# A written-out order of work: its clock refitted, its pacing table refined, its opening reordered

## The chip, the cores and the metric

The kernel runs on one core of a Trainium2 chip. A core has five engines with instruction queues of their own: TensorE (PE: matmuls, with weight loads shown apart as PEld), VectorE (DVE), ScalarE (ACT), GpSimd (POOL) and SyncE (SP, which here issues nearly all DMAs). Each engine works through its queue strictly in the order in which the program was written and waits, at the head of the queue, for semaphores that others raise. The metric is the device time of one execution in microseconds (us), smaller being better.

## The reference

The input `x` has 8192 rows of 448 numbers. Two branches start from its layernorm, and their product is added to `x`:

```python
def _A_ref(x, w1, b1, w2, b2):          # a spectral layer
    Xf = rfft2(x, axes=(1, 2))           # H = 1, so an FFT along the 8192 rows
    z = Xf.reshape(B, H, Wf, NB, BS)     # 4 blocks of 112 channels
    hr = relu(zr @ w1[0] - zi @ w1[1] + b1[0]);  hi = relu(zi @ w1[0] + zr @ w1[1] + b1[1])
    or_ = hr @ w2[0] - hi @ w2[1] + b2[0];       oi_ = hi @ w2[0] + hr @ w2[1] + b2[1]
    or_, oi_ = softshrink(or_, 0.01), softshrink(oi_, 0.01)
    return irfft2(or_ + 1j * oi_)

def _B_ref(x, w_gate, w_up, w_down):     # a GLU: 448 -> 1792 -> 448
    return (_gelu(x @ w_gate) * (x @ w_up)) @ w_down

xn = _layernorm(x)
return x + _A_ref(xn, ...) * _silu(_B_ref(xn, ...))
```

## The kernel before

All products are made in float16 from operands split into a high and a low half, three matmuls for each product, and the larger products go through a scheme of sums and differences (seven products in place of eight) whose operands DVE, ACT and POOL prepare.

**Stages.** The 8192 rows are worked off in 16 chunks of 512 (`NG`), the 1792 hidden columns in two passes `p` of 8 and 6 tiles of 128 (`PF`). The opening (`begin`, `begin1`, `weights`, `ffn`) takes chunks 0 and 1 with plain products (`plain`): for each hidden tile `f`, 22 matmuls of 512 columns, which need the split of that tile's weights (`gu_split`, event `("w", f)`). Chunks 2 to 15 of pass 0 and all of pass 1 use the seven-product form (`chunk`, `unit`, then `down` or `down2`). Between these products PE gets the matmuls of the spectral layer: the first FFT stage (`stage1`), the block MLP of phase 2 (`group`), the last stage of phase 3 (`tiles3`).

**The opening's weights.** `WS` is a ring of three buffers (tile `wst`) of 17 x 128 floats a partition. `begin` takes one for tile 0, `weights` one for tile 1, `gu_loads` one for each later tile. A first-round load (`in_gu`) fills only 8 x 128 of the 17 x 128, 512 KB in all, and the buffer comes free (`WS.put`) when `gu_split` has read it. Hidden tiles are grouped in blocks `BLK` with one power-of-two scale each: tile 0, tile 1, then pairs. The scale of a block needs the largest weight of both its tiles: DVE reduces each tile (`fm` or `fx`), PE turns the result (`bd<-ident,fx`), DVE reduces it (`mxr`), PE spreads it (`bd<-ident,mxr`), DVE computes the scale (`fx`, `fh`, `fc`, `fe`), and only then can ACT write the high halves (`wt<-wst,fc`). A block begins after the scales of the block before it. The second round (`gu_combs`, loads `in_raw`, 1088 KB each) prepares the seven-product form of the same tiles (`gu_comb`).

**Chunk 1 stage.** `chunk1(c)`, started at `T1 + (c - 2) * DT` of the planner's time, makes layernorm, the split and the sums of chunk c (`factors`), and writes them to the DRAM buffer `xts`; `xt_load` brings them back transposed (`DMA_TRANSPOSE xta<-xts` and `xtb<-xts`, issued by SP), and the seven-product part of chunk c starts on PE when its `xta` has landed.

**What sets the order.** The whole program is written by a planner that runs when the kernel is built. `Pace` keeps a clock: tasks are Python generators in a heap by time; each `V.`, `S.`, `G.`, `T.` or `Q.` call goes through `Pace.issue`, which computes when the operation would start (`start`: the engine is free, `ready`: operands are written, plus 0.12 us) and end (`cost`: a formula by engine, width and source), notes that, and emits the instruction. So the planner's times decide only one thing on the chip: which instruction stands before which in each queue. `Pace.clear` holds optional work back while the engine is late or a due instruction is near. `Either.call` (used as `B`, DVE or POOL) estimates the end on both engines and takes POOL when `ends[1] + self.by < ends[0]`, with `by = 0`. The cost model knows that a DVE operation with two SBUF inputs and a POOL operation collide (`port`): the later one is charged what is left of the earlier one. `STEPS` is a table by planner time: a value for DVE or ACT pacing, one added to the landing of DMAs (second value; third for `clear`), and a factor on the estimated durations of ACT, DVE and POOL. `END2` and `END3` spread phases 2 and 3 over fixed planner times and are not touched.

**The start of the opening.** SP issues x rows 0 and 2, weight tile 0 (512 KB), x rows 1 and 3. PE runs 13 matmuls on ones (`keep(13, 512)`, tile `gl`), whose results are overwritten, then waits. In `begin`, DVE's queue is: statistics of rows 0 and 2 (`moments`), the reduction of both halves of weight tile 0 in one instruction, the statistics of row 3, the `mxr` reduction, `normal(0)` and `normal(2)`, then the scale, the two low halves, and the copy of the first transposed rows; the copy of the second is ACT's.

Of the kernel before, what the change touches and what calls it, by code (L numbers as in the profile page):

```python
# [42 lines left out]
STEPS = ((0, 2.75, 0.05, 1), (100, 2.5, 0.15, 1.05), (175, 3, 0.2, 0.98), (250, 2.75, 0.05, 1), (325, 2.5, 0.05, 1), (400, 3.0, 0.1, 1.04), (475, 2.5, 0.05, 1), (550, 3.5, 0.05, 1), (700, 3.25, 0.3, 1), (775, 3.0, 0.3, 0.995), (850, 2.75, 0.05, 0.96), (925, 2.75, 0.05, 1.06), (1150, 2.5, 0.15, 0.995), (1450, 3, 0.1, 0.99), (1525, 2.75, 0.05, 1.02))  # L43
# [6 lines left out]
class Event:  # L50
    def __init__(self):
        self.done, self.waiting = False, []


class Pace:
# [4 lines left out]
    def __init__(self):  # L60
        self.now, self.last, self.n, self.heap = 0.0, 0.0, 0, []
        self.free, self.seen, self.dma = {"SP": 0.7, "ACT": 0.7, "DVE": 0.7, "POOL": 0.7, "PE": 1.0}, {}, 1.75
        self.port = {"DVE": [], "POOL": []}
        self.due = {"DVE": [], "ACT": []}
        self.late = False

# [72 lines left out]
    def ready(self, ap, write, engine):  # L139
        name, lo, hi = self.region(ap)  # L140
        return max((t + 0.12 for a, b, w, t, e in self.seen.get(name, ())
                    if (write or w) and e != engine and a < hi and lo < b), default=0.0)

    def note(self, ap, write, t, e):
# [4 lines left out]
        was.append((lo, hi, write, t, e))  # L149

    def quiet(self, ap):
        return max((x[3] for x in self.seen.get(ap.tensor.name, ())), default=0.0)

    def start(self, e, out, ins):
        outs = [out] if out.space != bass.MemoryType.DRAM else []
        ins = [i for i in ins if i.space != bass.MemoryType.DRAM]
        return outs, ins, max([self.now, self.free.get(e, 0.0)] + [self.ready(i, False, e) for i in ins]
                              + [self.ready(o, True, e) for o in outs])

    def issue(self, e, op, out, ins, run):  # L160
        outs, ins, start = self.start(e, out, ins)
        if e == "SP" or op == "dma_start":
            size = (outs or ins)[0].nbytes()
            self.dma = max(self.dma, start) + size / (320e3 if start > 10.0 else 400e3)
            if start < 10.0:
                self.free[e] = start + 0.46
                end = self.dma + 0.9
            elif op == "dma_start_transpose":
                self.free[e] = start + 1.15 + size / 380e3
                end = max(self.free[e] + 2.6, self.dma + 1.5)  # L170
            else:
                self.free[e] = start + 0.5
                end = max(start + 2.2 + size / 240e3, self.dma + 1.5) + (self.step(start)[1] if outs and start > 100.0 else 0.0)
        else:
            end = start + self.cost(e, op, start, out, ins) * (1.0 if e == "PE" else self.step(start)[3])
            self.free[e] = end
            if self.shares(e, op, out, ins):
                self.port[e] = self.port[e][-11:] + [(start, end)]
        for i in ins:
            self.note(i, False, end, e)  # L180
        for o in outs:
            self.note(o, True, end, e)
# [15 lines left out]
    def shares(self, e, op, out, ins):  # L198

        n, sb, psum = self.wide(out, ins)  # L200
        return e == "POOL" or e == "DVE" and n >= 32 and not psum and (sb >= 2 or op == "tensor_scalar" and sb > 0)

    def cost(self, e, op, start, out, ins):
# [8 lines left out]
        if e == "POOL":  # L212
            t = 0.7 if n < 8 and op == "tensor_tensor_pow" else 0.2 + 0.0023 * n
        elif n < 32:
            return 0.17
        elif psum or sb < 2 and op != "tensor_scalar":
            half = psum == len(ins) == 1 and op == "tensor_copy" and ins[0].dtype == F16
            return 0.14 + (0.00054 if half else 0.00107) * (n + 60 * (extra > 0))
        else:
            t = (0.12 + 0.00112 * n if sb >= 2 else 0.15 + 0.0008 * n) + 0.06 * (extra > 0)  # L220
        other, ahead = ("POOL", 0.15) if e == "DVE" else ("DVE", 0.0)
        return t + max([b - start - ahead for a, b in self.port[other] if a <= start < b] + [0.0])
# [17 lines left out]
class Either:  # L240
# [5 lines left out]
    def __getattr__(self, op):  # L246
        def call(out, *args):
# [4 lines left out]
            return getattr(self.engines[ends[1] + self.by < ends[0]], op)(out, *args)  # L252
# [249 lines left out]
def afno_geglu_kernel(ctx, tc, x, gu, raw, wd, mlp, b1, b2, c_m, c_mt, c_small, c_rows, out):  # L502
# [126 lines left out]
    WS = ring(wp, [128, SL * 128], F32, "wst", 3)  # L629
# [197 lines left out]
    T1, DT = 85.0, 34.5  # L827


    def gu_loads(fs, again):  # L830
        for f in fs:
            t = yield from WS.get()
            if f < 4 and not again:
                yield 2.5 + 2.5 * f

            n = (SL if again else 8) * 128
            Q.dma_start(t[:, 0:n], (raw if again else gu)[f])
            EV["wst", f, again] = t if again else t[:, 0:n].rearrange("p (s c) -> p s c", s=8)
# [51 lines left out]
    def gu_block(b):  # L890
# [23 lines left out]
        for i in range(n):  # L914
# [5 lines left out]
            WS.put(t)  # L920
# [1522 lines left out]
    def begin():  # L2443

        w = yield from WS.get()
# [12 lines left out]
        Q.dma_start(w[:, 0:8 * 128], gu[0][:, 0:8 * 128])  # L2458
# [14 lines left out]
        keep(13, 512)  # L2473
# [6 lines left out]
        t = EV["wst", 0, 0] = w[:, 0:8 * 128].rearrange("p (s c) -> p s c", s=8)  # L2480
# [48 lines left out]
        def leave1(a, b):  # L2529
# [4 lines left out]
            def rest():  # L2534
# [3 lines left out]

        moments(0)
# [4 lines left out]
        V.tensor_reduce(mx, t[:, 0:8].rearrange("p (i k) f -> p i (k f)", i=2), axis=AXIS.X, op=ALU.max,  # L2544
                        apply_absolute_value=True)
# [10 lines left out]
        normal(0)  # L2556
        cast(0, 0, xss[0])
        normal(2)
        cast(0, 2, xss[1])
        variance(1)  # L2560
        variance(3)
        root(2, 2)
        turn(banks[0], 0, xss[0], 0)
# [3 lines left out]
        turn(banks[1], 2, xss[1], 0)  # L2567
# [192 lines left out]
```

## Time and profile before

| | us |
|---|---|
| median of 3 runs (lowest, highest) | 1761.59 (1759.45, 1762.22) |
| profiled execution, device time | 1758.21 |
| its span, first to last instruction | 1756.4 |
| PE busy, share of the span | 1715.7, 98% |
| DVE / ACT / POOL busy | 1418.7 / 1113.9 / 751.5 |
| mean granted TensorE clock | 0.993 |

The page's busy time of an engine is the union of its instructions' spans. A matmul at half the granted clock counts as busy, so PE can lose time in two ways: idle, and busy at a clock below 1.00. The views by windows give both for any stretch; the list of waits names what ended PE's idle time; the chain of waits follows the last instruction back to the first. Times in these views count from the start of the span.

### The profile page before, as it was taken

To read this page: it belongs to the slowest core of one execution; us is meant where nothing else is said; L and a number is where in the kernel's file an instruction comes from. 1 tells how busy PE (TensorE), PEld (TensorE's weight loads), DVE (VectorE), ACT (ScalarE), POOL (GpSimd) and SP (SyncE) were. 2 spreads that over 40 slices of the span, in tenths; PEclk is the share of its full clock that TensorE was granted. 3 is DMA by queue.
4 is the path that set the end of the run, shared out by engine and by line. 5 is a ranking of instruction groups with operands and counts; after the bars stand their busy time and mean duration, and the time that the engine had idled before them with its cause. 6 is when DMAs were issued, how large, how long until landed. Compare 5 with 4: busy or idle time off the path is not lost.

```text
span 1756.4 us, 40962 instructions
## 1 busy us (share of the span) xinstructions
PE 1715.7 (98%) x15645; PEld 1435.9 (82%) x15645; DVE 1418.7 (81%) x2606; ACT 1113.9 (63%) x2279; POOL 751.5 (43%) x1083
## 2 busy tenths in 40 slices
PE   8998999999999999999999999999999999999997
PEld 4445677777777998999999989999899989889886
DVE  7898797777778877788887778888888887787787
ACT  6566676576676566778777666777676666333333
POOL 2277675566554564344333344432233432222222
PEclk9999999999999999999999999999999999999999
DMA  6428888887678653253445775445555545999996
GB/s 212 146 83 277 247 258 267 227 249 206 195 246 232 168 124 83 60 121 93 107 110 180 191 171 123 119 109 133 136 131 139 132 100 131 302 292 301 274 311 224
DMA packets 438308, 316.62 MB, mean 180 GB/s; under 512 B 305792, under 2 KB 409600, under 8 KB 436320
## 3 DMA queue, kind: packets, MB, share of 16 engines
q1 hardware_dynamic: 437824, 313.99, 63.6%
q8 instruction: 122, 2.00, 0.5%
q14 instruction: 74, 0.61, 0.1%
q10 hardware_dynamic: 288, 0.03, 0.0%
HBM read 137.93 MB, written 108.25 MB: 140 GB/s over the span
## 4 chain that ended last, share of the span: by engine, by line
PE 84%; DVE 7%; DMA 3%; ACT 3%; issue 2%; SPq 1%; POOL 1%; DVEq 0%; ACTq 0%; POOLq 0%
PE bd L235 34%; PE bx L235 29%; PE by L235 21%; DVE wt L235 1%; DVE u L235 1%; SPq L235 1%; DVE h L235 1%; DMA wst<-in_gu 1%; DMA prt<-th 1%; DVE va L235 1%; DMA xtb<-xts 1%; ACT h L235 1%; DVE o L235 0%; DMA vt<-va 0%; ACT o L235 0%
## 5 line engine op out<-in xcount | busy, mean ns | idle before, releaser
L235 PEld LDWEIGHTS <-wt 128*128 128x128 f16 x9142 | 887.2, 98 | 173.8 <-issue 19.4
L235 PE MATMUL bx<-xta,wt 128*128 128x256 f16 (+1 forms) x2819 | 355.5, 276 | 3.5 <-DMA xta<-xts 2.5
L235 PEld LDWEIGHTS <-h 128*128 128x128 f16 x2711 | 258.8, 98 | 73.5 <-DVE h L235 1.5
L235 PE MATMUL by<-xtb,wt 128*128 128x256 f16 x2080 | 255.7, 273 | 2.4 <-DVE by L235 1.3
L235 PE MATMUL bd<-dw,h 128*128 128x448 f16 (+1 forms) x1536 | 243.2, 306 | 0.0
L235 PE MATMUL bx<-xtb,wt 128*128 128x256 f16 x1248 | 153.2, 273 | 2.4 <-DVE v L235 2.3
L235 POOL TENSOR_TENSOR wt<-wt 128x256 f32<-128x256 f32 x81 | 63.0, 778 | 209.8 <-DVE wt L235 198.7
L235 PE MATMUL by<-xta,wt 128*128 128x256 f16 (+1 forms) x899 | 126.4, 285 | 2.7 <-ACT wt L235 1.9
L235 DVE TENSOR_TENSOR by<-bx,u 128x512 f32<-128x512 f32 x104 | 72.3, 695 | 43.4 <-PE bx L235 36.3
L235 ACT ACTIVATE u<-by,fc 128x512 f32<-128x512 f32 (+1 forms) x118 | 73.5, 635 | 47.9 <-PE by L235 47.0
L235 PE MATMUL bd<-dw,wt 128*128 128x224 f16 (+1 forms) x816 | 98.2, 264 | 3.6 <-DVE left L235 3.2
L235 PE MATMUL bx<-left,wt 128*128 128x256 f16 x816 | 100.0, 273 | 0.3 <-ACT by L235 0.3
L235 ACT COPY u<-by 128x512 f32<-128x512 f32 x104 | 60.7, 583 | 51.0 <-PE by L235 50.4
L235 ACT CAST h<-wt 128x512 f16<-128x512 f32 (+1 forms) x128 | 68.5, 536 | 36.1 <-DVE wt L235 29.1
L235 DVE TENSOR_TENSOR v<-bx,u 128x512 f32<-128x512 f32 x104 | 71.1, 684 | 16.1 <-PE bx L235 15.2
L235 DVE SCALAR_TENSOR_TENSOR left<-bd,ms,left 128x448 f32<-128x448 f32 x96 | 64.2, 678 | 22.5 <-PE bd L235 22.0
L235 ACT COPY by<-bx 128x512 f32<-128x512 f32 x104 | 60.1, 578 | 32.9 <-PE bx L235 32.6
L235 POOL TENSOR_TENSOR t<-h 112x256 f32<-112x256 f32 (+1 forms) x36 | 30.0, 832 | 114.3 <-ACT h L235 93.1
L235 PE MATMUL bd<-w2t,wn 113*128 113x112 f16 (+1 forms) x1152 | 78.1, 212 | 0.7 <-DVE wn L235 0.3
L235 PE MATMUL bd<-wt,h 128*128 128x224 f16 x603 | 72.2, 259 | 0.8 <-DVE h L235 0.7
L235 DVE SCALAR_TENSOR_TENSOR u<-by,fc,u 128x512 f32<-128x512 f32 (+1 forms) x86 | 55.4, 658 | 21.5 <-PE by L235 11.9
L235 PEld LDWEIGHTS <-wn 113*128 113x128 f16 (+1 forms) x1152 | 69.1, 97 | 3.8 <-POOL wn L235 0.6
(275 smaller groups left out, 3707.9 us busy)
## 6 DMA issues: line engine op xcount, KB each, us to landing
xts<-sx SPq DMA_DIRECT2D x32, 480.0 KB, 4.1
x<-in_x SPq DMA_DIRECT2D x17, 896.0 KB, 6.6
wst<-in_raw SPq DMA_DIRECT2D x14, 1088.0 KB, 7.0
t<-ysb SPq DMA_DIRECT2D x64, 224.0 KB, 3.5
prt<-th SPq DMA_DIRECT2D x64, 224.0 KB, 3.3
vt<-va SPq DMA_DIRECT2D x256, 56.0 KB, 2.1
left<-prt SPq DMA_DIRECT2D x64, 224.0 KB, 3.8
u<-t SPq DMA_DIRECT2D x32, 448.0 KB, 5.7
```

What stands on the lines that cost most here:

```text
L235: return self.pace.issue(self.name, kind, out, ins, lambda: fn(out, *args, **kw))
```

## The change

**1. The opening.** `keep(13, 512)` becomes `keep(22, 512)`. The reduction of weight tile 0 is cut into its two halves (`widest(0)`, `widest(1)`), and the normalisation and the casts of rows 0 and 2 go between them. Transposes of the high halves, the low half of row 0 (now POOL) and of row 2 (DVE) move ahead of the scale; both copies of transposed rows are DVE's, ahead of the second half of the weight split on ACT. The first four planner events of the opening are set at `early`. Two later low halves may go to either engine (`B` for `V`).

**2. Staging of the first-round weights.** The three buffers become one tile `raws`; for the first round it is cut into six half-size places (`near`), so that tiles 0 to 5 have a place at once; tiles 6 and 7 wait for the reading of tiles 0 and 1 only. The second round gets a full buffer when both first-round tiles in it are read.

**3. The planner's clock.** One delay from producer to consumer of 0.12 us becomes a delay by producer (`LATE`), an engine is free a little before its operation's result (`OVER`), accesses to one PSUM bank by two engines count as a conflict even when both read, the eight most recent SP transfers bound the next (`lanes`), a DMA's rate depends on its shortest run, POOL has a formula by kind of operation, and a collision of DVE and POOL now also pushes back operations planned already on the other engine (`push_on`).

**4. The table.** `STEPS` has 75 rows for 15 and a fifth column, added to `by` in `Either.call`; `T1, DT` go from 85.0, 34.5 to 84.0, 34.0.

```diff
-STEPS = ((0, 2.75, 0.05, 1), (100, 2.5, 0.15, 1.05), ... (1525, 2.75, 0.05, 1.02))
+STEPS = ((0, 2.75, 0.05, 0.97, 0.0), (15, 2.75, 0.05, 0.97, 0.0), (25, 2.75, 0.05, 1.0, 0.3), (35, 2.75, 0.05, 1.0, 0.3), (45, 2.75, 0.05, 1.07, 0.0),
...
+ (375, 2.5, 0.05, 1.04, -0.3),
...
+ (575, 3.5, 0.05, 1.0, 0.0),
...
+ (775, 3.0, 0.05, 1.0, -0.3), (800, 3.0, 0.05, 1.0, -0.3), (825, 3.0, 0.05, 1.0, -0.5),
...
+ (925, 2.75, 0.05, 1.06, 0.0),
...
+ (1275, 1.75, 0.05, 1.025, -0.2),
...
+ (1375, 1.75, 0.05, 1.025, -0.4),
...
+ (1675, 2.75, 0.05, 0.94, 0.1), (1700, 2.75, 0.05, 0.94, 0.1), (1725, 2.75, 0.05, 0.94, 0.4))
+LATE = {"PE": 0.2, "ACT": 0.045, "DVE": 0.045, "POOL": 0.045, "SP": 0.04}
+OVER = {"PE": 0.0, "ACT": 0.085, "DVE": 0.07, "POOL": 0.03}
@@ ready
-        return max((t + 0.12 for a, b, w, t, e in self.seen.get(name, ())
+        write = write or ap.space == PSUM
+        return max((t + LATE[e] for a, b, w, t, e in self.seen.get(name, ())
@@ start
+        lane = [self.lanes[-8]] if e == "SP" and len(self.lanes) > 7 else []
@@ new
+    def push_on(self, e, start, end):
+        by, before = None, 0.0
+        for k, (a, b, marks) in enumerate(self.port[e]):
+            if a > start:
+                by = end - (0.15 if e == "DVE" else 0.1) - a if by is None else by - max(0.0, a - before)
+                if by <= 0.0:
+                    return
+                self.port[e][k], before = (a + by, b + by, marks), b
+                for x in marks:
+                    x[3] += by
+        if by is not None:
+            self.free[e] += by
@@ charge, out of issue
-                self.free[e] = start + 0.5
-                end = max(start + 2.2 + size / 240e3, self.dma + 1.5) + ...
+                slow = turned or min(self.run_of(a) for a in (out, ins[0])) < 512
+                self.dma = max(self.dma, start) + size / (210e3 if slow else 330e3)
+                self.free[e] = start + (1.0 + size / 305e3 if turned else 0.6)
@@ cost
-            t = 0.7 if n < 8 and op == "tensor_tensor_pow" else 0.2 + 0.0023 * n
+            if n < 8:
+                t = 0.35 + 0.19 * n if op == "tensor_tensor_pow" else 0.25
+            elif sb < 2:
+                t = 0.18 + 0.00085 * n
+            else:
+                t = 0.18 + 0.0019 * n if out.dtype == F16 else 0.17 + 0.00217 * n
-            t = (0.12 + 0.00112 * n if sb >= 2 else 0.15 + 0.0008 * n) + 0.06 * (extra > 0)
+            t = (0.12 + 0.00109 * n if sb >= 2 else 0.13 + 0.0008 * n) + 0.06 * (extra > 0 and sb > 1)
@@ Either.call
-            return getattr(self.engines[ends[1] + self.by < ends[0]], op)(out, *args)
+            by = self.by + self.pace.step(self.pace.now)[4]
+            return getattr(self.engines[ends[1] + by < ends[0]], op)(out, *args)
@@ staging
-    WS = ring(wp, [128, SL * 128], F32, "wst", 3)
+    raws = wp.tile([128, 3 * SL * 128], F32, name="raws")
+    whole = [raws[:, SL * 128 * k:SL * 128 * (k + 1)] for k in range(3)]
+    near = [whole[f // 2 % 3][:, 1024 * (f % 2):1024 * (f % 2) + 1024] for f in range(8)]
+    WS = Slots(pace, [])
@@ gu_loads
-            t = yield from WS.get()
-            if f < 4 and not again:
-                yield 2.5 + 2.5 * f
+            if again:
+                t = yield from WS.get()
+            else:
+                t = near[f]
+                if f < 4:
+                    yield 2.5 + 2.5 * f
+                elif f > 5:
+                    yield ev("read", f - 6)
+                    yield pace.ready(t, True, None)
@@ gu_block
-            WS.put(t)
+            done("read", f)
+            if f % 2 and f > 1:
+                yield ev("read", f - 1)
+                WS.put(whole[f // 2 % 3])
@@ begin
-        keep(13, 512)
+        keep(22, 512)
         root(0, 2)
-        V.tensor_reduce(mx, t[:, 0:8]...)
+        widest(0)
         sums(1)
+        normal(0)
+        cast(0, 0, xss[0])
+        normal(2)
+        cast(0, 2, xss[1])
+        widest(1)
         squares(1)
+        turn(banks[0], 0, xss[0], 0)
         T.matmul(big[0:2, 0:128], upper(fx)[:, :, 0], identb, start=True, stop=True)
         keep(2, 256)
+        turn(banks[1], 2, xss[1], 0)
+        low(G, 0, 0, xss[0])
         moments(3)
...
+        turn(banks[0], 0, xss[0], 1)
+        low(V, 0, 2, xss[1])
         V.tensor_scalar(mxa, big[:, 128:130], unit_ ** -2, 2.0 ** -30, op0=ALU.mult, op1=ALU.max)
         scales(0)
         S.activation(d[:, 0, 0:4], t[:, 0:4], AF.Copy, scale=scale(0, 0))
         turn(banks[1], 2, xss[1], 1)
         V.tensor_copy(xT[:, :, 0:128], turned(banks[0]))
+        V.tensor_copy(xT[:, :, 128:256], turned(banks[1]))
+        S.activation(d[:, 0, 4:8], t[:, 4:8], AF.Copy, scale=scale(0, 1))
         stage1_at(0, first[0])
-        S.copy(xT[:, :, 128:256], turned(banks[1]))
```

More of the change, by code (lines that the diff above doesn't have):

```diff
@@ L2443, in begin @@
     def begin():
-        w = yield from WS.get()
+        w = near[0]
         x4 = EV["x4", 0] = yield from X4.get()
@@ L2697, in weights @@
         yield combs
-        for f in near:
+        for f in all0:
             yield ev("comb", f)
```

126 lines of the change are left out of this document (70 added, 56 removed).

## The prediction, as put on record before the changed kernel ran

> **What bounds the kernel now.** The page says which engine sets the time, and the view by windows says where that engine loses any. The windows were cut at the places where the granted clock changes and where PE has gaps. Columns: window, its length, then for each engine its busy time with its instructions, PE's granted clock, DMA share, GB/s.
>
> ```profile
> span 1756.4 us, 40962 instructions
> PE 1715.7 (98%) x15645; PEld 1435.9 (82%) x15645; DVE 1418.7 (81%) x2606; ACT 1113.9 (63%) x2279; POOL 751.5 (43%) x1083
> ```
> ```profile
> 5.54:8.96 3.42, 1.11 (x6) 0.35 (x5) 1.55 (x3) 0.87 (x3) 1.73 (x6) 1.00 0.99 356
> 8.96:12.37 3.41, 3.19 (x19) 1.55 (x18) 3.03 (x11) 3.03 (x6) 2.30 (x4) 0.50 1.03 423
> 12.37:15.78 3.41, 3.41 (x16) 1.83 (x15) 2.92 (x6) 2.24 (x6) 0.62 (x4) 0.50 0.29 117
> 15.78:39.00 23.22, 22.76 (x135) 12.28 (x132) 17.68 (x32) 16.98 (x45) 2.79 (x4) 1.00 0.70 230
> 39.00:42.00 3.00, 0.69 (x5) 0.22 (x4) 2.18 (x9) 2.04 (x6) 2.38 (x6) 1.00 0.00 0
> 43.10:46.50 3.40, 3.40 (x12) 1.33 (x11) 3.40 (x6) 2.28 (x6) 1.15 (x1) 0.50 0.03 2
> 56.00:62.00 6.00, 3.01 (x18) 1.36 (x18) 5.57 (x13) 5.55 (x12) 2.02 (x2) 0.85 0.30 76
> 60.20:63.60 3.40, 2.93 (x10) 1.01 (x8) 3.36 (x6) 3.05 (x8) 1.25 (x2) 0.50 0.00 0
> 62.00:155.00 93.00, 90.23 (x441) 42.79 (x440) 84.15 (x173) 62.39 (x119) 57.43 (x89) 0.99 0.47 157
> 155.00:176.00 21.00, 17.78 (x138) 14.22 (x138) 18.24 (x39) 12.07 (x27) 12.86 (x27) 0.92 0.81 234
> 176.00:350.00 174.00, 172.90 (x1319) 128.15 (x1318) 139.70 (x264) 117.86 (x234) 106.30 (x192) 1.00 0.85 248
> 350.00:650.00 300.00, 300.00 (x2438) 237.30 (x2437) 231.81 (x456) 201.25 (x394) 176.01 (x319) 1.00 0.74 206
> 650.00:1650.00 1000.00, 988.28 (x10207) 906.45 (x10205) 814.35 (x1453) 645.07 (x1352) 355.17 (x396) 1.00 0.57 151
> 1650.00:1743.00 93.00, 90.30 (x814) 78.44 (x813) 75.98 (x118) 33.18 (x58) 27.42 (x27) 1.00 0.89 288
> 1743.00:1757.00 14.00, 3.94 (x36) 3.23 (x34) 8.60 (x17) 3.20 (x6) 1.44 (x1) 0.74 0.38 132
> ```
>
> PE is the bound: from 350 to 650 us it has no gap at all. The change touches no product, so it can win only what PE loses. That is 1756.4 - 1715.7 = 40.7 us of idle time, plus half of the busy time at clock 0.50. It sits at both ends: up to 62 us, again at 155 to 176, then 1.10 + 11.72 + 2.70 = 15.5 us in thin gaps over 1567 us, and a tail in which PE has nothing left. Everything below is a sum against the profiled execution, 1758.21 us (its span and 1.8 us around it); the median of the runs shown, 1761.59, is 3.4 us above it, and the sum is carried over to the median. About 0.2%, 3.5 us, is what a measurement of this kernel can tell from no change.
>
> **Part 1, the first matmuls.** The timeline of the opening (start, duration, engine, operation; in brackets idle time and releaser):
>
> ```profile
> 7.47 1.22 DVE L235 TENSOR_REDUCE fx<-wst 128x2 f32<-128x1024 f32 x1 [1.86 <-DMA wst<-in_gu]
> 7.63 0.20 POOL L235 TENSOR_TENSOR st<-st 128x2 f32<-128x2 f32 x1
> 8.63 0.63 DVE L235 BATCH_NORM_STATS2 st<-x 128x6 f32<-128x448 f32 x1
> 9.57 0.91 DVE L235 TENSOR_SCALAR x<-x,st 128x448 f32<-128x448 f32 x2
> 10.71 2.79 PE L235 MATMUL bd<-ident,xs 128*128 128x128 f16 x16
> 11.03 1.33 ACT L235 ACTIVATE wt<-wst,fc 128x512 f16<-128x512 f32 x2
> 14.53 1.55 PE L235 MATMUL by<-xta,wt 128*128 128x256 f16 x7
> ```
>
> POOL has the row scales at 7.83, but DVE normalises at 9.57, behind the reduction and the statistics of row 3. With the reduction in halves (1.22 / 2 = 0.61, an estimate from that row) `normal(0)` can start at 7.47 + 0.61 = 8.1, and the first transpose 10.71 - 9.57 = 1.14 later, at 9.2: 1.5 us earlier. The scale goes the other way. DVE then has 0.91 for two rows, 0.61 for the second half, 0.8 of statistics, about 0.25 for `mxr`, and a low half of about 0.6, now ahead of the scale; the weight split on ACT starts at about 12.0 instead of 11.03. The split of the first half takes 1.33 / 2, the two copies on DVE end near 13.2, so the first GLU matmul starts near 13.3 instead of 14.53: 1.2 us gained, between 0 (a DVE instruction more in the way) and 2.5.
>
> The nine added warm-up matmuls lie in a stretch where PE idles (1.11 us busy from 5.54 to 8.96). Thirteen take 4.98 us in all:
>
> ```profile
> 1.46 4.98 PE L235 MATMUL bx<-gl 128*128 128x512 f16 x13 [1.46 <-DVE gl L235]
> ```
>
> At that rate nine are 3.4 us and end at 9.9, 0.7 us into the transposes; at the full clock granted from 5.54 they end sooner. What they buy is the clock: 12.37 to 15.78 ran at 0.50 for 3.41 us, of which half is lost, 1.7. The new GLU matmuls reach into about half of that window, so I take 0.8, from -0.7 to 1.7. Part 1 is 2.0, from -0.7 to 4.2.
>
> On this step the Trainium skill, "TensorE: Matmul & The Clock Gate", section "What's actually happening", says that a window of about 3.4 us of idling halves the clock and a busy one restores it, but also that the windows run free of the kernel's start. The 3.41 us steps above agree with the first. By the second, the 0.8 us would come in some runs and not in others, and the sum would be 0.8 us smaller.
>
> **Part 2, the weights of the opening.** The gaps at 39 and 56 us, followed along the chain of waits and in SP's queue:
>
> ```profile
> 5.72 10.92 SPq L235 DMA_DIRECT2D wst<-in_gu  x2
> 25.77 0.34 SPq L235 DMA_DIRECT2D wst<-in_gu  x1
> 30.84 14.98 SPq L235 DMA_DIRECT2D wst<-in_gu  x3
> 47.88 0.33 SPq L235 DMA_DIRECT2D wst<-in_raw  x1
> ```
> ```profile
> 30.84 6.93 DMA wst<-in_gu
> ```
>
> Tile 5's load could leave only at 30.84, when DVE had read tile 2 out of its buffer; it landed 6.93 us later, was reduced, and PE, idle for most of 39 to 42, went on when the scale was there. Tiles 6 and 7 were late in the same way and made the gaps from 56 us. With six places the loads of tiles 3, 4 and 5 leave by about 11 us, tiles 6 and 7 after the reading of tiles 0 and 1 (in the rows the buffers of these two came free at about 16 and 26 us, when the loads of tiles 3 and 4 left). PE asked for the block of tiles 4 and 5 at 39 us: the data will be there. What can still be late is DVE, busy 17.68 of 23.22 us from 15.78 to 39. At stake: 2.31 idle in 39 to 42, half of 3.40 at half clock, 2.99 idle in 56 to 62, half of 2.93: 1.70 + 1.47 + 5.30 = 8.5 us. I take 7.5, from 3 (the scale chains of later tiles still wait on DVE) to 8.5. The two loads moved forward, 512 KB each, go ahead of the down weights in SP's queue, which nothing in the opening reads before tile 7 is split. Parts 1 and 2 bring PE to the end of the opening 9.5 us earlier.
>
> **Part 3, the gate at 155 us.** There PE waits for chunk 2's transposed rows:
>
> ```profile
> 144.41 3.98 SPq L235 DMA_DIRECT2D xts<-xs  x5
> 148.49 4.36 SPq L235 DMA_TRANSPOSE xta<-xts  x1
> ```
> ```profile
> 155.81 1.44 PE L235 MATMUL bx<-xta,wt 128*128 128x256 f16 x6 [2.46 <-DMA xta<-xts]
> ```
>
> PE at 146 instead of 155.8 is worth nothing unless this transfer moves as well. It stands behind five writes of chunk 3, and behind chunk 2's sums, which DVE, ACT and POOL make among the second-round weights. Two things move it: `T1` starts the stage 1 us earlier, and the second-round loads, first issued at 47.88, can start some 15 us earlier, so that DVE does this work in time that it now idles (5.5 us in 15.78 to 39, the difference of that row); after 62 us it is 90% busy. I let `xta` come 6 us earlier, between 1 (T1 alone) and 9.5 (as much as PE); what it lacks, 3.5, is a longer wait. Up to here 6 us are won, from 1 to 12. From 155 to 176 PE idles 3.22 us on DVE and on this transfer; I change nothing there.
>
> **Part 4, the rest.** The list of PE's waits from 176 to 1743 us (total, times, longest):
>
> ```profile
> PE bd L235 <- DVE left L235: 3.2, 4, 1.7
> ...
> PE bd L235 <- POOL wn L235: 0.2, 1, 0.2
> ```
>
> The 15.5 us are single lapses of this kind, each where the planner put a matmul before an operand that came a little late. A better clock removes such lapses and shuffles others in. How many of them it hits no row of before can show. The bounds are 15.5 (all gone) and -8 (half as many again). I take 6, two in five, because the new terms are of the kind that the rows ask for: for one, POOL's 128x256 difference planned at 0.2 + 0.0023 x 256 = 0.79 before and 0.73 now, near the 0.778 of its row below, which holds collisions. The tail after 1743 is a chain of DVE, ACT and stores that the change doesn't shorten: 0, from -2 to 2.
>
> **Sum:** 6 + 0 + 6 + 0 = 12 us. 1758.2 - 12 = 1746.2 for a profiled execution, 1761.6 - 12 = 1749.6 for the median.
>
> **Rivals.** *The gate holds.* `xta` comes only T1's 1 us earlier: PE then waits 8.5 us longer at 155 and nearly all of parts 1 and 2 is lost there. For it speaks that DVE is 90% busy from 62 to 155. Gain 1 us and 0 to 6 later: 1754.6 to 1760.6. The variant in which the new clock is no better on the chip than the old ends here too.
>
> *Everything comes.* `xta` moves with PE, and two thirds of part 4 goes: 9.5 + 10 = 20 us, 1741.6. For it speaks that no later stretch is gated by anything but single waits.
>
> *Slower: work pushed to POOL.* The table's fifth column is negative for 375 to 575, 775 to 925 and 1275 to 1675 us, 750 of 1757, so that POOL is taken though it ends up to 0.5 us later. The groups by form (count, then busy us and mean ns of one, idle before) give the price of the commonest such difference on either engine:
>
> ```profile
> L235 POOL TENSOR_TENSOR wt<-wt 128x256 f32<-128x256 f32 x81 | 63.0, 778 | 209.8 <-DVE wt L235 198.7 <-ACT h L235 8.7 <-PE bd L235 0.5
> L235 DVE TENSOR_TENSOR wt<-wt 128x256 f32<-128x256 f32 x111 | 54.2, 488 | 3.3 <-POOL wt L235 1.4
> ```
>
> and, from the timeline of the opening,
>
> ```profile
> 58.59 2.02 POOL L235 TENSOR_TENSOR sx<-x,sx 128x448 f16<-128x448 f32 x2 [4.16 <-ACT sx L235]
> 58.62 1.03 DVE L235 TENSOR_SCALAR fc<-fh 128x2 f32<-128x2 f32 x1
> ```
>
> Here a DVE instruction on two numbers a row took 1.03 us beside a POOL operation. Of the 111 DVE differences 750 / 1757 are 47, each 0.78 us on POOL: 37 us of added POOL work. Where half of it reaches PE, through the moved result or a blocked DVE, 18 us are lost and the change is 18 - 12 = 6 slower: 1768. It decides from a third (12 us). Against it: in those stretches POOL's results mostly feed products that come much later, and PE has one wait on POOL from 176 us on (0.2 us). The Trainium skill, "SBUF — State Buffer", section "Who interferes with whom", says that a DVE instruction with two SBUF inputs and a POOL instruction that reads SBUF exclude each other, the later one being blocked; the rows agree for small DVE operations, and by it a shift to POOL frees DVE less than the counts say.
>
> **Chances.** Forecast, 1743 to 1754: 0.40. Everything comes, 1734 to 1743: 0.21. The gate holds, 1754.6 to 1760.6: 0.24, half of it within 0.2% of before. Slower, 1762 to 1775: 0.15. Faster by over 0.2% (below 1758.1): 0.40 + 0.21 + 0.12 = 0.73; within 0.2%: 0.13 with a share of the slower case; slower: 0.14. The range, 1738 to 1764, leaves out the far ends of the second and the last case; the forecast's own is 1743 to 1754.
>
> **What would show it.** Part 1: first GLU matmul (`by<-xta,wt`) before 13.5 us, clock 1.00 from about 9 us on. Part 2: all eight first-round loads issued by 30 us, no gap of over 1 us and no half clock between 35 and 65. Part 3: the wait on `xta<-xts` near 6 us (2.5 before) and PE past it near 150. Part 4: idle time from there to PE's last matmul near 10 us rather than 15.5. I am wrong if the wait on `xta` is 10 us (the gate), if PE waits on POOL or on stretched DVE operations after 375 us, or if the gaps of part 2 stay with the loads early, which would put DVE's scale chain in their place.

## The result, and the profile after

| | before | changed |
|---|---|---|
| median (lowest, highest) of 4 runs, us | 1760.64 (1759.45, 1762.22) | 1738.55 (1737.31, 1740.49) |
| span of the profiled execution | 1756.4 | 1735.5 |

The ratio is 0.9875 with a 95% interval of 0.9858 to 0.9892: 22 us faster, where 12 were forecast. The time lies 0.6 us above the low end of the range, 1738 to 1764, and outside the forecast's own 1743 to 1754: it is a time of the rival "everything comes" (1734 to 1743).

The page's first lines and the view by windows, cut as nearly as it can be where the kernel before was cut (window, length, busy time of PE, PEld, DVE, ACT and POOL, PE's clock, DMA share, GB/s):

```profile
span 1735.5 us, 40997 instructions
PE 1709.6 (99%) x15654; PEld 1434.6 (83%) x15654; DVE 1404.9 (81%) x2438; ACT 1097.0 (63%) x2240; POOL 937.6 (54%) x1291
```
```profile
5.54:8.96 3.42, 3.42 (x13) 1.24 (x11) 1.28 (x3) 0.71 (x3) 1.57 (x6) 1.00 0.96 352
8.96:12.37 3.41, 3.02 (x26) 1.97 (x26) 3.23 (x11) 2.37 (x6) 2.60 (x4) 1.00 1.03 422
12.37:15.78 3.41, 3.29 (x26) 2.22 (x24) 2.87 (x7) 2.39 (x8) 1.39 (x6) 1.00 1.03 419
15.78:39.00 23.22, 21.93 (x124) 11.10 (x122) 21.45 (x41) 19.12 (x51) 4.93 (x7) 1.00 0.64 227
39.00:42.00 3.00, 3.00 (x16) 1.37 (x14) 3.00 (x5) 1.61 (x3) 2.59 (x6) 1.00 0.86 278
56.00:62.00 6.00, 6.00 (x31) 2.80 (x29) 5.34 (x10) 4.81 (x8) 2.40 (x4) 1.00 0.00 0
...
160.00:350.00 190.00, 187.17 (x1446) 140.66 (x1445) 164.78 (x302) 131.40 (x262) 123.52 (x214) 1.00 0.85 257
350.00:650.00 300.00, 298.99 (x2432) 236.39 (x2431) 228.59 (x417) 186.83 (x369) 195.53 (x327) 1.00 0.71 194
650.00:1650.00 1000.00, 995.60 (x10283) 913.85 (x10281) 796.43 (x1329) 637.95 (x1328) 497.91 (x568) 1.00 0.59 155
1650.00:1726.00 76.00, 74.50 (x668) 64.34 (x666) 62.43 (x96) 29.70 (x52) 30.16 (x30) 1.00 0.84 284
```

The two gaps of the opening are gone (3.00 of 3.00 and 6.00 of 6.00 us busy), the clock is not halved before PE's last matmul, and in the thousand microseconds from 650 on PE idles 4.4 us instead of 11.7. Not all is better: from 160 to 350 us PE idles 2.8 us and from 350 to 650 1.0, where before had 1.1 (from 176 on) and none. POOL is 186 us busier, DVE 14 less. The wait on `xta<-xts`, 2.5 us before, is no longer among PE's waits.

Since the products are the same, a second measure locates the gain. For each execution the useful matmuls (warm-ups left out) were summed in the order in which PE ran them, at the pace of back-to-back ones (0.109 us for 256 columns). The **lead** at a place is how much earlier this execution reached a given sum than the kernel before's profiled execution; places are named by the time at which before reached them. It is worked out from PE's records, and two executions of the same instructions differ by up to 3.5 us in it (last section). Nor is the last place the end: the spans of e1, e6 and e8 are 3.4, 7.5 and 16.0 us longer than before's, where their last leads are -7.0, -11.1 and -19.6.

| place (us of before) | 33.7 | 61.7 | 108.8 | 176.1 | 388.9 | 589.7 | 945.5 | 1252.4 | 1707.7 | 1746.5 |
|---|---|---|---|---|---|---|---|---|---|---|
| changed kernel | 0.7 | 8.5 | 9.2 | 14.2 | 12.3 | 11.5 | 12.2 | 16.2 | 20.5 | 21.1 |

So 9 us come from the opening, 5 at the gate near 156 us, where 3.5 were expected to be lost, 3 are given back by 590, and nearly 10 come after that.

### The profile page after: what moved, and what is told of

Read it like the earlier page. It is cut to its first block, busy times and chain, and to the rows that moved or that the text cites. A ratio compares the mean times of both kernels' runs of the same rounds, so it can differ in the third digit from the quotient of the medians.

```text
span 1735.5 us, 40997 instructions
## 1 busy us (share of the span) xinstructions
PE 1709.6 (99%) x15654; PEld 1434.6 (83%) x15654; DVE 1404.9 (81%) x2438; ACT 1097.0 (63%) x2240; POOL 937.6 (54%) x1291
## 4 chain that ended last, share of the span: by engine, by line
PE 44%; DVE 3%; POOL 2%; ACT 1%; issue 1%; SPq 0%; DMA 0%; DVEq 0%; ACTq 0%; POOLq 0%
PE bd L288 19%; PE bx L288 14%; PE by L288 11%; DVE wt L288 1%; DVE th L288 0%; POOL wn L288 0%; POOL h L288 0%; DVE va L288 0%; POOL wt L288 0%; DVE h L288 0%; SPq L288 0%; DVE g L288 0%; ACT h L288 0%; DVE o L288 0%; DVE t L288 0%
## 5 line engine op out<-in xcount | busy, mean ns | idle before, releaser
L288 POOL TENSOR_TENSOR wt<-wt 128x256 f32<-128x256 f32 x133 | 107.2, 806 | 158.8 <-DVE wt L288 151.5
L288 POOL TENSOR_TENSOR t<-h 112x256 f32<-112x256 f32 (+1 forms) x34 | 26.0, 765 | 125.8 <-ACT h L288 104.9
L288 POOL TENSOR_TENSOR h<-wt,h 128x256 f16<-128x256 f32 (+1 forms) x65 | 71.4, 1106 | 15.5 <-ACT h L288 15.4
```

Of the source, the lines that this page charges most:

```text
L288: return self.pace.issue(self.name, kind, out, ins, lambda: fn(out, *args, **kw))
```

## The experiments

All compare with the kernel before on the same chip. Theory A at the start: the staging of part 2 opens the gate. Its rival B: the refitted clock does. After the first four runs two others stood: C, the table is a fit to this one plan, and any other plan lacks the gain; D, the refitted clock makes better plans in general. Leads, by the same places:

| place | 33.7 | 61.7 | 108.8 | 176.1 | 388.9 | 589.7 | 945.5 | 1252.4 | 1707.7 | 1746.5 |
|---|---|---|---|---|---|---|---|---|---|---|
| e1 staging alone | -1.3 | 5.1 | -2.5 | -0.4 | -3.7 | -4.3 | -5.7 | -6.3 | -8.4 | -7.0 |
| e2 clock alone | 0.2 | 3.7 | -0.8 | 2.8 | -3.0 | -7.2 | -10.4 | -8.5 | -17.8 | -16.1 |
| e3 old table | 1.1 | 6.8 | 3.7 | 6.7 | -0.3 | -4.9 | -11.5 | -9.2 | -11.9 | -11.2 |
| e4 old clock | -1.1 | 8.1 | 8.0 | 4.5 | 2.0 | -9.7 | -14.5 | -13.7 | -18.2 | -16.7 |
| e6 before, nudged | 0.2 | 0.2 | 0.2 | 0.2 | 0.4 | 0.4 | -3.8 | -10.1 | -12.5 | -11.1 |
| e7 column off | 0.9 | 8.7 | 9.4 | 13.9 | 11.9 | 8.4 | 8.1 | 11.1 | 6.4 | 4.4 |
| e8 opening and staging | -2.2 | 4.2 | -1.9 | 0.5 | -0.4 | -2.0 | -6.3 | -11.0 | -20.4 | -19.6 |
| e9 wide nudge up | -0.6 | 6.9 | 7.9 | 11.7 | 8.8 | 8.0 | 8.6 | 4.2 | 3.5 | -3.1 |
| e10 wide nudge down | 1.1 | 8.6 | 9.6 | 13.9 | 11.9 | 11.1 | 11.1 | 13.1 | 14.5 | 7.9 |
| e11 13 warm-ups | 0.0 | 7.7 | 8.7 | 12.5 | 11.0 | 10.1 | 10.9 | 15.3 | 19.6 | 20.2 |
| e12 column on before | -0.8 | 0.4 | -0.1 | -1.3 | -1.5 | -1.5 | -1.5 | -2.9 | -3.2 | -2.7 |

### e1: the staging alone

```diff
 # the kernel before, with
-    WS = ring(wp, [128, SL * 128], F32, "wst", 3)
+    whole = [raws[:, SL * 128 * k:SL * 128 * (k + 1)] for k in range(3)]
+    near = [whole[f // 2 % 3][:, 1024 * (f % 2):1024 * (f % 2) + 1024] for f in range(8)]
...
```

> The kernel before with part 2 alone (six half-size places for the first-round weights). Theory A, the staging opens the gate at 155 us: PE's work is some 9 us ahead by 62 us, the second-round weights start earlier too, the wait on xta<-xts stays under 3 us and the lead after it is 9 or more; time 1747 to 1752. Rival B, the refitted clock opens the gate (order of SP's queue): the lead at 62 us is the same 9, but PE waits 8 us or more on xta<-xts, the lead after it is 1 to 3; time 1757 to 1760.

1757.74 us, ratio 0.9993 (0.9982 to 1.0004): no gain, and neither theory as it was put: the time is in B's range, but PE had no wait on chunk 2's `xta`, and the lead at 61.7 was 5.1 for the 9 of both. (The profiled execution, 1761.56, is the slowest of ten, so its leads look worse than the kernel is.) The loads were early, seven of the eight issued by 17 us and the last at 27.10 (SP's timeline):

```profile
5.97 11.25 SPq L235 DMA_DIRECT2D raws<-in_gu  x5
27.10 0.34 SPq L235 DMA_DIRECT2D raws<-in_gu  x1
```

With that the gaps of the opening closed for the most part (30 to 66 us, before and then e1): PE idles 2.46 us for 5.30, no clock is halved, and from 33.7 to 61.7 us the lead grows by 6.4. Then come PE's two waits of over 1.5 us between 10 and 160 us:

```profile
30.00:66.00 36.00, 30.70 (x145) 13.63 (x144) 29.18 (x54) 23.59 (x57) 12.26 (x18) 0.91 0.44 139
```
```profile
30.00:66.00 36.00, 33.54 (x170) 14.83 (x169) 32.43 (x62) 29.65 (x67) 13.73 (x21) 1.00 0.39 126
```
```profile
59.32 0.82 PE L235 MATMUL bx<-xta,wt 128*128 128x512 f16 x3 [1.71 <-ACT wt L235]
...
94.15 0.59 PE L235 MATMUL by<-wt,wt 128*128 128x512 f16 x1 [3.65 <-DVE u L235]
```

The first, what is left of the gap at 56, is on tile 7's high half, which ACT wrote after a piece of the second round that stood before it (ACT's timeline). No wait on a scale chain is left there; the one on `fx`, 3.5 us, is tile 0's, at 9.34. The second, with half clock from 92.99 us on for 6.83, took the rest of the lead.

```profile
55.75 1.25 ACT L235 ACTIVATE raws<-raws,fc 128x1152 f32<-128x1152 f32 x1
...
57.90 0.72 ACT L235 ACTIVATE raws<-raws,fc 128x512 f32<-128x512 f32 x1
58.65 0.62 ACT L235 CAST wt<-raws 128x512 f16<-128x512 f32 x1
```

The buffers were the limit at 39 and 56 us; with them gone, what DVE and ACT have before them in their queues is the next one.

### e2: the refitted clock alone, with the old table

```diff
 # the kernel before, with part 3
+LATE = {"PE": 0.2, "ACT": 0.045, "DVE": 0.045, "POOL": 0.045, "SP": 0.04}
+OVER = {"PE": 0.0, "ACT": 0.085, "DVE": 0.07, "POOL": 0.03}
...
```

> The kernel before with part 3 alone (the refitted clock, with the old table of 15 rows and no fifth column). The buffers still hold tile 5 back, so both theories expect the gaps at 39 and 56 us to stay. Theory A: no lead over before at 155 us, and a gain only where single lapses go: 1753 to 1759. Rival B: xta<-xts lands earlier by some us, the lead after it is 3 to 5; 1748 to 1754. If the clock without its table only shuffles the lapses: 1759 to 1765.

1775.57 us, ratio 1.0094 (1.0072 to 1.0116): slower by 16 us, beyond every case. The gaps at 39 and 56 us stayed, as expected (PE idles 4.47 us from 30 to 66, clock 0.91). Whether the refitted clock is the truer model of the chip no run measures; by itself it made a worse program.

### e3 and e4: all but the table, all but the clock

```diff
 # e3: the changed kernel, with
-STEPS = ((0, 2.75, 0.05, 0.97, 0.0), ... 75 rows)
+STEPS = ((0, 2.75, 0.05, 1), (100, 2.5, 0.15, 1.05), ... 15 rows)
-            by = self.by + self.pace.step(self.pace.now)[4]
 # e4: the changed kernel, with the old Pace (no LATE, OVER, lanes, push_on; old DMA and POOL costs)
```

> The changed kernel with the old table of 15 rows and no fifth column (parts 1, 2, 3 and T1 stay). If the clock and the staging carry the gain, the lead of 10 at 62 us and of 14 after the gate stay, and most of the later 7: 1739 to 1743. If the later 7 us are the table's: 1745 to 1750, with the lead stuck near 12 to 14 from 180 us on.

1772.11 us, ratio 1.0075 (1.0054 to 1.0096).

> The changed kernel with the old clock (parts 1, 2, the new table and T1 stay). Theory A: lead of 10 at 62 us, no long wait on xta<-xts, 12 or more after it; the later lapses come back: 1743 to 1749. Rival B: PE waits 6 us or more on xta<-xts, lead after it 3 to 6: 1751 to 1757.

1777.93 us, ratio 1.0105 (1.0078 to 1.0132). Both are slower than the kernel before, and beyond every case of their expectations. They have most of the opening's lead (6.8 and 8.1 at 61.7) and lose it, e4 in single long waits such as these:

```profile
PE bx L235 <- ACT gl L235: 8.0, 1, 8.0
PE by L235 <- DVE u L235: 6.0, 3, 4.7
...
PE bx L235 <- DMA xta<-xts: 2.1, 1, 2.1
```

On the gate neither theory holds whole. With the old clock `xta` landed at 147.80 instead of 155.76, so the refitted clock is not needed for 8 us of it, against B; but the staging alone brought 3.3 us (e1, 152.47), against A, and in e4 PE still waited 2.1 us and the lead fell to 4.5. For the rest of the program neither A nor B was the question: the new clock without its table, and the new table without its clock, are each worse than the old pair.

### e5 to e7: nudges, and the column

```diff
 # e5: the changed kernel
-(575, 3.5, 0.05, 1.0, 0.0), (600, 3.5, 0.05, 1.0, 0.0)
+(575, 3.5, 0.05, 1.01, 0.0), (600, 3.5, 0.05, 1.01, 0.0)
 # e6: the kernel before
-(550, 3.5, 0.05, 1)
+(550, 3.5, 0.05, 1.01)
 # e7: the changed kernel, fifth column 0 in every row from 375 on
```

> The changed kernel with the duration factor of two of the table's 75 rows (575 and 600) at 1.01 for 1.00: the same program up to about 575 us, where it is 11.5 us ahead of the kernel before; 9.6 of the gain come after that. Theory C, the gain after 575 us is a fit of the table to exactly this plan: most of it goes with the nudge, as a one per cent change of an estimate reshuffles all later instructions; 1743 to 1752. Theory D, the refitted clock makes better plans in general: a nudge costs less than 2 us either way; 1737 to 1741.

1739.47 us, ratio 0.9874 (0.9859 to 0.9888). It looked like D, but was hardly a test: of DVE's instructions three stood elsewhere.

> The kernel before with one of its 15 rows (550) at 1.01 for 1: the same program up to about 550 us. Theory C says that the old table was fitted to its plan too: slower than before by 3 to 12, 1763 to 1772. If a plan is as good as its neighbours: within 3 of before, on either side.

1767.76 us, ratio 1.0031 (1.0018 to 1.0044), 5.5 us slower, as C has it. This nudge moved about a thousand of DVE's 2606 instructions.

> The changed kernel with the fifth column at 0 in all rows from 375 us on, so no preference for POOL there: the same program up to about 375 us, 12.3 us ahead. If the shift to POOL itself earns the later gain (DVE relieved), POOL is some 100 us less busy, DVE more, and the later gain of 9 goes: 1746 to 1754. If the shift is no more than one more way to fit the plan, the loss is that of the nudge. If it costs (the rival with blocked DVE), the time falls below 1738.

1753.8 us, ratio 0.9956 (0.9939 to 0.9972). The stretch from 1275 to 1675, of the changed kernel and then of e7:

```profile
1275.00:1675.00 400.00, 399.79 (x3936) 362.73 (x3935) 315.84 (x496) 211.60 (x415) 189.15 (x209) 1.00 0.74 211
```
```profile
1275.00:1675.00 400.00, 392.40 (x3847) 354.11 (x3845) 328.73 (x536) 206.97 (x405) 141.26 (x153) 1.00 0.71 206
```

Without the column POOL does 48 us less there, DVE 13 more, and PE idles 7.6 us instead of 0.2. That fits "DVE relieved", but e7 also moves some thousand DVE instructions, so it can't be told from a shuffle by itself; e9, e10 and e12 were made for that. It gives no support to the slower rival: the plan with more work on POOL is the faster one.

### e8: opening and staging, old clock and old table

```diff
 # the kernel before, with parts 1 and 2
-        keep(13, 512)
+        keep(22, 512)
+        widest(0)
...
+    near = [whole[f // 2 % 3][:, 1024 * (f % 2):1024 * (f % 2) + 1024] for f in range(8)]
...
```

> The kernel before with parts 1 and 2, old clock, old table, old T1. Staging alone was 5 us ahead at 61 us and lost it at 94. If the prediction's step is right that the two parts bring 9.5 by 62 us without the clock, the lead there is 8 to 10; after the gate 4 to 8 of it are left. By theory C the later plan is a reshuffle of a fitted one and gives 5 to 10 back: 1754 to 1762.

1772.8 us, ratio 1.0059 (1.0038 to 1.0079), a miss for the 8 to 10 at 62 us. The clock was halved for 6.83 us from 19.23 on, which costs 3.4 of the lead, and the wait of 1.7 us on tile 7's high half is there as in e1 (the stretches of e8):

```profile
16.00:39.00 23.00, 21.17 (x105) 10.83 (x105) 17.75 (x31) 14.92 (x39) 2.63 (x5) 0.85 0.67 227
39.00:62.00 23.00, 20.87 (x111) 9.27 (x112) 19.73 (x41) 17.23 (x38) 9.86 (x14) 1.00 0.31 107
```

From 33.7 to 61.7 the lead grows by 6.4, as in e1; the halved clock need not be this plan's, since e9's execution has one there with the changed kernel's own opening (last section).

### e9 and e10: two wide nudges of the changed kernel

```diff
 # the changed kernel, rows 575, 600, 625, 650, 675, 700: fourth value + 0.01 (e9), - 0.01 (e10)
```

> The changed kernel with the factor of the six rows from 575 to 700 raised by 0.01. The two-row nudge moved only some 60 of DVE's instructions and so tested little; this one moves about as many (2700 lines of DVE's order) as the nudge of the old table did, which lost 11 us of span. Theory C (the table is a fit to this one plan): the 9.6 us after 575 go for the most part, span 1743 to 1750. Theory D (the refitted clock plans better, whatever the shuffle): within 3 us of the changed kernel, 1737 to 1742.

1758.89 us, ratio 0.9994 (0.9985 to 1.0004): the whole gain is gone, though the program is the same up to 575 us and was 8.0 us ahead there; the span, 1757.8, is beyond C's 1750.

> The same six rows lowered by 0.01: a second, independent shuffle from 575 us on. Theory C: again 5 to 12 us lost, 1743 to 1751. Theory D: 1736 to 1742. Two shuffles that differ by more than 5 us between them would show how wide the spread of plans is.

1750.59 us, ratio 0.9947 (0.9929 to 0.9964). These moved about 900 and 1000 of DVE's instructions, as many as e6. PE's waits after 575 us, of the changed kernel, e9 and e10:

```profile
PE bd L288 <- DVE left L288: 1.6, 4, 0.6
PE bx L288 <- ACT by L288: 1.3, 2, 1.0
```
```profile
PE bd L288 <- DMA mt<-c_mt: 5.5, 2, 3.2
PE bd L288 <- DVE bd L288: 4.6, 3, 2.6
PE bd L288 <- DVE left L288: 2.0, 4, 1.0
PE bd L288 <- POOL h L288: 1.8, 1, 1.8
```
```profile
PE bd L288 <- DMA mt<-c_mt: 4.8, 1, 4.8
PE bx L288 <- DVE v L288: 2.8, 2, 1.6
PE bd L288 <- POOL h L288: 2.6, 2, 1.7
```

Most of these waits differ from plan to plan, but the longest is the same in both, on `mt`, in the last 20 us (PE's rows of e9, then of e10, and the longest wait of SP's queue in the 22 and 9 us before, of e9, then of e10):

```profile
1738.31 1.31 PE L288 MATMUL bd<-u,mt 128*128 128x448 f16 x6 [2.30 <-DMA mt<-c_mt]
1742.78 5.51 PE L288 MATMUL bd<-u,mt 128*128 128x448 f16 x24 [3.16 <-DMA mt<-c_mt]
```
```profile
1732.66 2.42 PE L288 MATMUL bd<-u,mt 128*128 128x448 f16 x6 [4.76 <-DMA mt<-c_mt]
```
```profile
SPq L288 <- POOL g L288: 10.5, 1, 10.5
```
```profile
SPq L288 <- DVE g L288: 5.4, 1, 5.4
```

SP's queue holds a store of `g` ahead of these loads, SP waits for `g` itself, and the loads leave late (at 1736.11 and 1728.11 the last ones); in the changed kernel the last one leaves at 1716.27 and PE does not wait. After the place 1707.7 both lose 6.6 us of lead, where the changed kernel wins 0.6; up to there e10 still gained on the kernel before (2.6 us from 389 on). Of the 22 and 13 us of span that the nudges cost against the changed kernel, these waits are 5.5 and 4.8; the rest is single lapses, and in e9 3.5 us that it was behind before the nudge. D falls as it was put (a cost under 3 us), and C stands for the size of the loss: 22 and 13 us of span for a one per cent change of an estimate.

### e11: 13 warm-ups in the changed kernel

```diff
-        keep(22, 512)
+        keep(13, 512)
```

> The changed kernel with 13 warm-up matmuls for 22. The prediction gave the nine 0.8 us, through the clock: at half clock again from 9 to about 16 us, first GLU matmul within 0.3 us of 13.08, and a lead over the kernel before that is 0.5 to 1.5 us smaller at 20 us. What comes later is a reshuffle of the whole plan, since the planner's time of PE changes: by theory C 1745 to 1755, by theory D 1738 to 1742.

1739.13 us, ratio 0.9880 (0.9864 to 0.9896), within the interval of the changed kernel. The reshuffle didn't happen: the order on DVE, ACT and POOL is the same to the instruction, and PE's and SP's too but for the nine, so this run prices the nine matmuls alone. The clock did what was expected (e11, then the changed kernel):

```profile
9.00:16.00 7.00, 6.69 (x39) 4.13 (x40) 5.54 (x16) 4.12 (x12) 3.53 (x9) 0.58 1.02 418
```
```profile
9.00:16.00 7.00, 6.49 (x53) 4.30 (x52) 6.28 (x17) 4.94 (x13) 4.21 (x9) 1.00 1.03 421
```

The lead at 33.7 is 0.7 smaller and 0.9 at the end, less than two executions of one program can differ by.

### e12: the column on the kernel before

```diff
 # the kernel before, rows of 1275 us and later
+(1275, 2.5, 0.15, 0.995, -0.2), (1375, 2.5, 0.15, 0.995, -0.4), (1450, 3, 0.1, 0.99, -0.4), (1525, 2.75, 0.05, 1.02, -0.4)
```

> The kernel before with the fifth column alone, at the changed table's values (-0.2, from 1375 us -0.4) from 1275 us on: the same program up to there. If the preference for POOL is what earns the late gain (DVE relieved in 1275 to 1675, where it falls from 326 to 316 us in the changed kernel), DVE falls by 8 us or more there and PE's idle time of 3.7 in that stretch halves: 1755 to 1759. If it needs the refitted clock: 1760 to 1768.

1759.47 us, ratio 0.9996 (0.9984 to 1.0008). From 1275 to 1675 it reads:

```profile
1275.00:1675.00 400.00, 396.11 (x3913) 359.54 (x3911) 319.13 (x515) 212.84 (x420) 161.84 (x177) 1.00 0.71 201
```

DVE was relieved by 7 us against before (326.14) and PE's idle time stayed, 3.9 for 3.7. With the old clock and table the preference for POOL earns nothing. It is also a plan with some 200 of DVE's instructions moved that costs nothing, against C in its strict form.

## Why the prediction was right in direction and short in size

The forecast's 12 us were 10 short, and that the time still fell inside the range, by 0.6 us, is luck. So is its falling among the times of "everything comes": that rival had no gain at the gate and 10 us in part 4, and the runs show 5 and 7.

**What bounds the kernel** was right: all of the gain is PE's idle time and half clock, and no part of the program became bound by another engine.

**Part 1** was right in its times: the first transpose at 9.44 (9.2 put), the weight split on ACT at 11.77 (12.0), the first GLU matmul at 13.08 (13.3), full clock from 9 us on; the warm-ups' 0.8 came out as 0.6 in the medians and 0.7 in the lead, neither clear of the noise. The lead is 1.7 at 15 us for the 2.0 of the sum, but 1.0 at 20 and 0.7 at 33.7; in between lies a wait that was not in the sum: PE idles 0.92 us at 17.20 for a low half that took DVE twice its time beside a POOL operation (DVE's, POOL's and PE's rows):

```profile
14.42 0.75 DVE L288 SCALAR_TENSOR_TENSOR wt<-raws,fc,wt 128x512 f16<-128x512 f32 x1
15.62 1.52 DVE L288 SCALAR_TENSOR_TENSOR wt<-raws,fc,wt 128x512 f16<-128x512 f32 x1
```
```profile
15.22 1.37 POOL L288 TENSOR_TENSOR xs<-x,xs 128x448 f16<-128x448 f32 x1 [1.69 <-ACT xs L288]
```
```profile
17.20 0.50 PE L288 MATMUL bx<-xta,wt 128*128 128x256 f16 x3 [0.92 <-DVE wt L288]
```

Rule and row agree here with what the prediction took from the Trainium skill, "SBUF — State Buffer", section "Who interferes with whom": both instructions have two inputs in SBUF. (The prediction's own row for it, `fc<-fh` at 58.62, has one and is not a case of it.) It is an example of the price that the slower rival named, in a place that the prediction did not name: the low half of another row, given to either engine by part 1 itself.

**Part 2** was right in amount and in its mechanism: 8.5 and 9.2 at 62 and 109 us for the 9.5 of parts 1 and 2 together, with all loads issued by 25.28 us, no gap over 1 us and no half clock from 35 to 65. The staging alone, with the old clock and table, gives 6.4 of its 7.5 between 33.7 and 61.7 (e1, and e8 again), so the gaps were the buffers' and not DVE's scale chain's. Wrong was to carry the 9.5 on to the gate as if nothing lay between: in the plans of e1 and e8 a wait of 3.65 us on DVE at about 94 us and the halved clock with it take the lead to below zero at 109. The changed kernel's longest wait there is 1.5 us; e4, with the new table and the old clock, keeps 8.0 at 109 us, e3, with the new clock and the old table, 3.7.

**Part 3** is the step that failed in size: it lost 3.5 us in the sum and won 5.0. `xta` was let come 6 us earlier, between 1 and 9.5; it landed at 142.14 instead of 155.76, 13.6 earlier, and PE, at 144.55, did not wait. SP's rows:

```profile
125.06 1.01 SPq L288 DMA_DIRECT2D xts<-sx  x1
...
128.29 1.77 SPq L288 DMA_DIRECT2D xts<-sx  x1
130.16 2.36 SPq L288 DMA_DIRECT2D prt<-th  x3
133.83 5.33 SPq L288 DMA_TRANSPOSE xta<-xts  x1
```

The last write of chunk 2 leaves at 128.29 instead of 141.75, and none of chunk 3's five writes stands before the transpose. The upper bound, "as much as PE", was no bound: the stage works ahead of PE, on other engines. How early it comes goes with how much DVE has done, most of it in time that it idled before (in the changed kernel 21.45 us busy of 23.22 from 15.78 to 39, and 21.86 of 23.00 from 39 to 62, for 17.68 and 18.60):

| | before | e1 | e8 | e2 | e4 | e3 | changed |
|---|---|---|---|---|---|---|---|
| DVE busy up to 128.3 us | 108.4 | 106.7 | 107.5 | 109.7 | 112.8 | 115.9 | 116.6 |
| landing of chunk 2's `xta` | 155.76 | 152.47 | 151.83 | 153.12 | 147.80 | 145.29 | 142.14 |

Before has its 117 us of DVE's work done at 141.8, when its last write leaves. The staging, alone or with the opening, and the clock alone bring 2.6 to 3.9 us; e1 and e8 do so with no more work done on DVE, since one write of chunk 3 stands before the transpose there instead of five. With parts 1, 2 and `T1` in place, the new table brings 8.0 (e4) and the new clock 10.5 (e3) of the 13.6. That DVE's work is the cause in these fits the table and is not shown by a run of its own; the share of `T1`, in both, is not known. The second-round loads left at 37.87 us, 10 us earlier where 15 were put.

The other half of the miss is a term that the sum put at nothing: "From 155 to 176 PE idles 3.22 us [...]; I change nothing there", in a row that also shows a clock of 0.92. Before, PE waits 2.46, 0.59, 0.44 and 1.24 us from 150 to 176 and runs 3.41 us at half clock from 155.73 on, 6.4 us in all (e6 and e12, the same program up to there, have such a stretch from 155.21 and 164.45 on). The changed kernel has no half clock there, and these waits:

```profile
148.12 1.25 PE L288 MATMUL bx<-xta,wt 128*128 128x256 f16 x10 [1.01 <-ACT by L288]
150.81 1.25 PE L288 MATMUL by<-xtb,wt 128*128 128x256 f16 x10 [0.34 <-DVE by L288]
```

The difference, 5.1 us, matches the 5.0 by which the lead grew from 109 to 176 us. With the 3.5 of the forecast that is 8.5 of the 9.1 us by which the lead at the end, 21.1, is above the 12 of the sum.

**Part 4**, 6 us, measured 6.9 from 176 us to the end with the tail, and its sign came true (PE idles 9.7 us from 160 us to its last matmul, for "near 10"). Its reason was wrong, so that the number fits is luck. "A better clock removes such lapses" is not borne out by e2, e3, e9 and e10, which have the refitted clock. From 389 us to the last place, five plans of the new clock lost 13.1, 10.9, 7.5, 11.9 and 4.0 us against the kernel before (e2, e3, e7, e9, e10), four of the old clock lost 3.3, 18.7, 19.2 and 11.5 (e1, e4, e8, e6), and e12, with the smallest shuffle of those, 1.2; the changed kernel won 8.8, and e11, the same plan, 9.2. The reading that fits is that the pair wins: a table whose rows suit the one plan that this clock makes with them. The old kernel's pair looks to be of the same kind (e6). That the table was fitted so is inferred from the nudges, not shown.

**The rivals.** The gate did not hold. POOL did not slow the later stretches. "The new clock is no better on the chip than the old" was filed with the gate's case; as the runs have it, it is true of the clock by itself and not of the clock with its table.

**What stays open.** Whether the refitted clock makes better plans on the average: ten plans spread from 1 to 19 us of loss, and the two groups overlap. Whether the late load of `mt` alone accounts for the end of e9 and e10: no run moved it. Which part of the late gain is the fifth column's: e7 lies among the shuffles. Undoing T1 alone, or the staging alone in the changed kernel, wasn't tried.

## What to carry to other kernels

Where a planner writes a static order, judge a change of its model by several plans, not by one: a one per cent nudge of one estimate that moves a thousand instructions cost 5 to 20 us of 1750 here, more than most terms of a sum. Before a nudged or ablated run is read as a price, compare the instruction orders; only a run like e11, with the same order on every other engine, prices one edit. When a gap is laid to a missing buffer, look at what is late next, there and 30 us further on, and when a transfer gates a stage, ask which engines prepare it and whether they idle earlier, not how much the waiting engine gains; and price the halved clock behind the wait along with the wait.

## What the runs showed of the hardware that was not expected

The same instructions give a different clock in different executions. Up to 575 us e9's program is the changed kernel's; from 15 to 39 us the one was granted 0.93 and the other 1.00 (the windows of e9, then of the changed kernel):

```profile
15.00:39.00 24.00, 22.71 (x122) 11.64 (x122) 20.89 (x39) 18.36 (x48) 5.43 (x6) 0.93 0.60 217
```
```profile
15.00:39.00 24.00, 22.70 (x130) 11.56 (x128) 22.23 (x43) 19.90 (x55) 5.49 (x7) 1.00 0.66 233
```

The 0.93 is one stretch of 3.41 us at half clock, from 19.58 on. e7, whose program is the changed kernel's up to 375 us, has such a stretch from 11.16 on, and the changed kernel, e5 and e10 have none up to 62 us. So the warm-ups kept the clock in four of these five executions, and in e7's it was halved in spite of them, without a smaller lead at 33.7, 0.9 (e7 from 9 to 16 us):

```profile
9.00:16.00 7.00, 6.70 (x43) 4.30 (x44) 6.36 (x17) 4.56 (x12) 4.36 (x9) 0.76 1.03 420
```

At the place 389 us e9 was 3.5 us behind the changed kernel with the same program, 1.3 of it by 33.7, about what half of the 3.41 us makes. So a difference of leads of that size between two profiled executions carries nothing; the medians are steadier (10 runs of e9 lie within 2.8 us). It agrees with what the page on the clock gate says of windows that run free of the kernel's start (the Trainium skill, "TensorE: Matmul & The Clock Gate", section "What's actually happening"); that the place of the windows is the cause here, no run shows.
